# The last 96 rows of w2 in 24 small transfers on partitions 0 to 31

## The chip, the cores and the metric

The kernel runs on one core of a Trainium2 chip. The metric is the device time of one execution in microseconds (us). Times of single executions, the profiled one among them, are compared with the median of several.

## What is computed

One decode step for two sequences: attention of 32 heads over a cache of 4096 positions, a two-layer network with relu beside it, and a gate that mixes the two.

```python
x = A_x                                             # [2, 1, 512]
g = sigmoid((x * gate_w).sum(-1, keepdims=True))
q = (x @ wq), 32 heads of 128
p = softmax(q @ k_cache.T / sqrt(128))              # k_cache, v_cache [2, 32, 4096, 128]
a = (p @ v_cache), heads joined, @ wo               # wo [4096, 512]
b = relu(x @ w1) @ w2                               # w1 [512, 1376], w2 [1376, 512]
out = g * a + (1 - g) * b
```

All inputs are bfloat16. The two caches are 64 MB each; w2 is 1.4 MB.

## The kernel before

**Streaming.** The caches are read in eight units of 8 MB each (64 KB on each of 128 partitions). Unit 0 and unit 7 of K come as halves, unit 7 of V too. Nearly all loads are issued by SP, in one queue, in the order of the code: w1, wq, ten transfers of K (L272), nine of V (L282), wo in two parts (L283, L284), then w2. Two one-off loads (x, two rows, and gate_w, one row) are issued by ACT (L265, L266). A K or V transfer waits until the buffer that it fills is read out. Every load increments a semaphore by 16 when it has landed.

**Stages.** `gate` makes the gate's values g and 1 - g (`gm`). `q_proj` makes q. `ffn_h` makes the hidden layer h on PE in eleven groups of four matmuls, each 128 hidden units by 2 sequences, from w1 in `kt`; DVE then applies relu and the factor 1 - g and writes `hT` (128 partitions x 11 groups x 2). Then 64 pieces of K are transposed by DVE (`k_turn`, L383) and multiplied by PE (`k_scores`, L404 and its helper L197). `softmax` follows; E and ET lie in `kt`. `spread(j)` writes the weights of job j into `ptm`, in four parts, on POOL, DVE and ACT; `v_unit(j)` multiplies them with V on PE; `v_extract(j)` brings the sum out on DVE into `X2[:, j]`. `o_gather` collects the heads, `project` multiplies with wo, and `wo_sum` adds its four parts to the result's PSUM tile `fin`.

**w2.** The 1376 hidden units are put on partitions as follows: units 0 to 1279 as ten groups (partition p has units 10p to 10p + 9), and an eleventh group from the last 128 units, 1248 to 1375. Its first 32 are there twice, so POOL sets `hT[0:32, 10, :]` to zero (L376). w2 comes in six transfers, all with 128 partitions: `w2a` (L285) is the eleventh group, 1 KB on each partition. It waits for the four parts of the last `spread`, `pt_8_0` to `pt_8_3`, for then `kt` is no longer read. `w2b` to `w2f` (L290) are the ten groups in five parts: 6144, 2560, 512, 512 and 512 bytes on each partition, with no wait of their own.

**The end.** After `project`, PE runs `ffn_f(10)` (the eleventh group, waits for `w2a`), `wo_sum`, `ffn_f(0)` to `ffn_f(7)` (waits for `w2b` at 0 and `w2c` at 6), half of group 8, and `ffn_last`, which waits for `w2d`, `w2e` and `w2f` in turn. Four copies by DVE and ACT (L576, L578) bring the result to `out_sb`, and SP writes it out (L292). SP's queue holds nothing else.

The engines run in the order in which the code adds to them; a wait holds up all that follows on its engine.

## Time and profile before

| | us |
|---|---|
| median of 3 runs (lowest, highest) | 344.14 (343.99, 344.16) |
| profiled execution, its own time | 344.06 |
| its span, first to last instruction | 342.8 |
| PE busy | 197.6 (58%) |
| DVE busy | 178.6 (52%) |
| ACT, POOL busy | 23.1, 19.9 |
| w2a, from issue to last landing | 30.4 |
| w2b to w2f, the same | 31.5 to 32.3 |

The span is the time between the first and the last instruction in the trace; the rest of the execution's time, 1.3 us, lies around it. A slice is a fortieth of the span, 8.6 us. A transfer is issued by an instruction on SP or ACT and then moved by sixteen DMA engines, each of which takes its share of the rows; the time from issue to landing holds the wait behind transfers that were issued earlier. The trace has a record for every packet (queue, start, duration, bytes, but not which of the sixteen engines) and for every increment of a semaphore, so the sixteen landings of a transfer can be seen one by one.

### The profile page before, as it was taken

The page shows a single profiled execution, that of the slowest core. Times are in us where ns is not written, and L with a number is a line of the kernel's source. Part 1 is how long each engine was busy: PE and PEld are TensorE (multiplying, and loading weights), DVE is VectorE, ACT ScalarE, POOL GpSimd, SP SyncE. Part 2 cuts the span into 40 slices and gives each one's busy share as a digit, 9 for nine tenths or more (in the row PEclk, how much of TensorE's full clock was granted, in tenths as well). Part 3 has the DMA queues.
Part 4 walks back from the last instruction along what each step waited for, and adds up shares of the span by engine and source line. Part 5 has one row for each costly group of instructions (what it writes and reads, how often), then busy time and mean ns, then how long its engine had stood idle before and what let it go on. Part 6 is the DMA issues. An engine that isn't in the chain of part 4 may idle for free.

```text
span 342.8 us, 2538 instructions
## 1 busy us (share of the span) xinstructions
PE 197.6 (58%) x1228; PEld 54.5 (16%) x972; DVE 178.6 (52%) x127; ACT 23.1 (7%) x71; POOL 19.9 (6%) x36
## 2 busy tenths in 40 slices
PE   0177329799969799699799337220706043150656
PEld 0141001111111111111111013100303011020231
DVE  2239059899799899698999562220100103020121
ACT  1040000000000000000000250000000000000000
POOL 8000000000000000000000040110100101000000
PEclk9999959989999999989999858755656758565787
DMA  8998989899998999998999999999999999999996
GB/s 348 428 489 369 482 375 482 382 474 451 400 489 375 422 444 467 392 459 386 471 436 428 461 398 417 449 459 413 444 413 446 421 436 451 405 468 390 425 404 243
DMA packets 4196, 145.61 MB, mean 425 GB/s; under 512 B 469, under 2 KB 986, under 8 KB 1242
## 3 DMA queue, kind: packets, MB, share of 16 engines
q1 hardware_dynamic: 4180, 145.46, 98.6%
q8 instruction: 8, 0.13, 0.2%
q14 instruction: 2, 0.02, 0.0%
q10 hardware_dynamic: 6, 0.00, 0.0%
HBM read 145.46 MB, written 0.00 MB: 424 GB/s over the span
## 4 chain that ended last, share of the span: by engine, by line
DMA 68%; DVE 15%; PE 13%; ACT 1%; issue 1%; POOL 0%; SPq 0%; DVEq 0%
DMA kv<-in_A_k_cache_dram 31%; DMA kv<-in_A_v_cache_dram 23%; DVE kt L383 13%; DMA kt<-in_B_w_dram 9%; PE PS L458 6%; DMA kv<-in_A_wq_dram 4%; PE PS L404 3%; PE PS L197 3%; ACT kt L425 1%; PE PS L330 1%; DVE mpad L410 1%; DVE kt L468 1%; POOL ptm L441 0%; DVE qbuf L464 0%; DVE kt L429 0%
## 5 line engine op out<-in xcount | busy, mean ns | idle before, releaser
L383 DVE STREAM_TRANSPOSE kt<-kv 128x2048 f32<-128x2048 f32 x64 | 141.2, 2274 | 22.4 <-DMA kv<-in_A_k_cache_dram 22.3
L404 PE MATMUL PS<-kt,qbuf 128*128 128x512 bf16 x256 | 105.7, 413 | 31.8 <-DVE kt L383 26.3
L197 PE MATMUL PS<-kt,qbuf 128*128 128x512 bf16 x256 | 105.1, 411 | 0.0
L458 PE MATMUL PS<-kv,ptm 128*32 128x512 bf16 x512 | 46.4, 539 | 79.2 <-DMA kv<-in_A_v_cache_dram 76.2
L464 DVE TENSOR_TENSOR qbuf<-PS,maskc 128x512 f32<-128x512 f32 x9 | 6.2, 692 | 109.0 <-PE PS L458 109.0
L404 PEld LDWEIGHTS PS<-kt,qbuf 128*128 128x128 bf16 x256 | 25.5, 100 | 139.9 <-DVE kt L383 72.8
L458 PEld LDWEIGHTS PS<-kv,ptm 128*32 128x32 bf16 x512 | 19.0, 129 | 105.1 <-issue 98.2
L441 POOL COPY ptm<-kt 32x512 bf16<-32x512 bf16 (+1 forms) x18 | 11.5, 638 | 268.5 <-DVE rsum L472 175.6
L357 ACT ACTIVATE qbuf<-PS 32x8 bf16<-32x8 bf16 x40 | 7.9, 196 | 134.0 <-PE PS L197 132.6
L445 ACT ACTIVATE ptm<-kt 32x512 bf16<-32x512 bf16 (+1 forms) x9 | 5.3, 604 | 99.9 <-PE PS L458 98.6
L468 DVE TENSOR_REDUCE kt<-qbuf 128x128 f32<-128x512 f32 x9 | 9.2, 1026 | 0.3
L425 ACT ACTIVATE kt<-PS,negm 128x512 bf16<-128x512 f32 x8 | 5.4, 700 | 30.5 <-DVE negm L421 30.5
L330 PE MATMUL PS<-kv,xTw 128*32 128x512 bf16 x32 | 3.6, 631 | 5.8 <-DMA kv<-in_A_wq_dram 5.8
L475 PE MATMUL PS<-rsum,sell 128*32 128x1 f32 x4 | 0.4, 197 | 10.1 <-DVE rsum L472 10.1
L429 DVE STREAM_TRANSPOSE kt<-kt 128x1024 bf16<-128x1024 bf16 x4 | 5.0, 1245 | 1.7 <-ACT kt L425 1.4
L345 DVE CAST qrow<-PS 128x256 bf16<-128x256 f32 x2 | 2.4, 1400 | 6.4 <-PE PS L330 6.4
L505 PE MATMUL PS<-kv,oW 128*2 128x512 bf16 x32 | 3.5, 603 | 1.3 <-DMA kv<-in_A_wo_dram 1.3
L297 PE MATMUL PS<-ident,x_sb 3*128 3x3 bf16 x4 | 0.3, 165 | 6.0 <-POOL s L227 6.0
L483 PE MATMUL PS<-kt,selx 128*32 128x128 f32 x18 | 3.3, 325 | 0.4 <-DVE kt L468 0.4
L230 POOL MEMSET ptm<- 128x4096 bf16 x1 | 3.5, 3501 | 0.0
L300 DVE COPY xT<-PS 128x12 bf16<-128x12 bf16 x1 | 0.2, 171 | 6.3 <-PE PS L297 6.3
L410 DVE TENSOR_REDUCE mpad<-PS 128x1 f32<-128x2048 f32 x1 | 2.3, 2293 | 2.2 <-PE PS L197 2.2
(64 smaller groups left out, 44.5 us busy)
## 6 DMA issues: line engine op xcount, KB each, us to landing
kv<-in_A_k_cache_dram SPq DMA_DIRECT2D x4, 4096.0 KB, 31.6
kv<-in_A_v_cache_dram SPq DMA_DIRECT2D x2, 4096.0 KB, 27.0
kv<-in_A_wq_dram SPq DMA_DIRECT2D x1, 4096.0 KB, 14.9
kv<-in_A_wo_dram SPq DMA_DIRECT2D x1, 3072.0 KB, 29.3
kt<-in_B_w_dram SPq DMA_DIRECT2D x1, 1376.0 KB, 5.7
kv<-in_A_wo_dram SPq DMA_DIRECT2D x1, 1024.0 KB, 31.4
kt<-in_B_w_dram SPq DMA_DIRECT2D x1, 768.0 KB, 31.9
kt<-in_B_w_dram SPq DMA_DIRECT2D x1, 320.0 KB, 32.3
```

What stands on the lines that cost most here:

```text
L197: return e.add_instruction(mybir.InstMatmult(start_tensor_calc=start, stop_tensor_calc=stop, tile_size=(128, 128), tile_position=(0, 0), l ...
L330: pe(lambda e, n=n, t=t: e.matmul(psf(32 * (n % 4), 32 * (n % 4) + 32, (QR_B + n // 4) * BANK, 512), lhsT=xTw[:, t, :], rhs=wq_sb[:, t, n ...
L357: act(lambda a, hq=hq: a.activation(out=qbuf[32 * hq:32 * hq + 32, g % 2, :, :, 32 + 32 * hq], in_=cols[32 * hq:32 * hq + 32, u4 // 2, 2 * ...
L383: dve(lambda v: v.transpose(out=dst, in_=pairs[:, h, 64 * rr:64 * rr + 64]), waits=([f"pe_sc_{i - NKT}"] if i >= NKT else ["pe_h"] if i == ...
L404: return e.matmul(args[0], lhsT=args[1], rhs=args[2], start=first, stop=last)
L410: dve(lambda v: v.tensor_reduce(out=mpad[:, 0:1], in_=psf(0, 128, 0, 2048), axis=AX.X, op=ALU.max), waits=["pe_sc_63", "c_mpad"], signal=" ...
L425: act(lambda a, bk=bk, e2=e2: a.activation(out=blocks[:, bk, :, 16 * e2:16 * e2 + 16], in_=psf(0, 128, bk * BANK, 512).rearrange("p (r n) ...
L441: pool(lambda e, args=args: e.tensor_copy(**args), waits=waits, signal=f"pt_{j}_{hq}")
L445: act(lambda e, args=args: e.activation(func=ACT.Copy, **args), waits=waits, signal=f"pt_{j}_{hq}")
L458: pe(lambda e, m=m, t=t: e.matmul(psf(32 * t, 32 * t + 32, V_B[j % 2] * BANK, 512), lhsT=ptm[:, j % 2, 4 * m:4 * m + 4, :, :], rhs=rows[:, ...
L464: dve(lambda e: e.tensor_tensor(out=Y.rearrange("p (c d) -> p c d", c=4), in0=psf(0, 128, V_B[u % 2] * BANK, 512).rearrange("p (c d) -> p ...
L468: dve(lambda e: e.tensor_reduce(out=X2[:, u, :], in_=Y.rearrange("p (c d) -> p d c", c=4), axis=AX.X, op=ALU.add), waits=[f"dve_y{u}"], si ...
```

## The change

The eleventh group is replaced by the last 96 units alone, 1280 to 1375, in four groups on fewer partitions: 32 units (1280 to 1311), twice 24 (the even and the odd ones of 1312 to 1359), and 16 (1360 to 1375). `hT` grows to 14 groups. Their w2 rows come in 24 transfers in place of `w2a`: eight with 4 partitions of 1 KB (partitions o, o + 8, o + 16, o + 24), eight with 3 partitions of 2 KB, and eight with 2 partitions of 1 KB. All increment `w2a`'s semaphore, and PE waits for 24 times 16. The first waits as `w2a` did. In bytes they are 96 KB in place of 128 KB. `w2b` to `w2f` are as they were, and stand behind them in SP's queue.

With this, `ffn_h` has 56 matmuls for 44 and four DVE instructions for two; POOL's memset is gone; `ffn_f` runs for groups 10 to 13 ahead of `wo_sum`, with 32, 24, 24 and 16 partitions. As w2's place in `kt` grows, five of the nine parts of `X2` move to a buffer of their own, and the result's staging tile takes the place of x.

```diff
+H_TAIL = ((32, 1280, 1), (24, 1312, 2), (24, 1313, 2), (16, 1360, 1))
...
-    hT = sb("hT", [128, 11, 2], dt.bfloat16)
-    out_sb = sb("out_sb", [2, 512], dt.bfloat16)
+    hT = sb("hT", [128, 14, 2], dt.bfloat16)
+    X2a = sb("X2a", [128, 5, 128], dt.float32)
+    out_sb = x_sb[0:2, :]
...
-    w2f = flat[:, 0:2816].bitcast(dt.bfloat16)
+    w2f = flat[:, 0:3584].bitcast(dt.bfloat16)
...
-    X2 = flat[:, 2944:4096].rearrange("p (u d) -> p u d", d=128)
+    X2b = flat[:, 3584:4096].rearrange("p (u d) -> p u d", d=128)
...
-    sp(lambda e: e.dma_start(w2[:, 10, :], B_w2[1248:1376, :]).then_inc(sem["w2a"], 16),
-       waits=[f"pt_8_{hq}" for hq in range(4)])
-
+    ready = [f"pt_8_{hq}" for hq in range(4)]
+    few = []
+    for r, n, row in ((10, 32, 1280), (11, 24, 1312), (13, 16, 1360)):
+        w = 2 if r == 11 else 1
+        src = B_w2[row:row + n * w, :].rearrange("(p w) n -> p (w n)", w=w)
+        few += [(w2f[o:n:8, 512 * r:512 * (r + w)], src[o:n:8, :]) for o in range(8)]
+    for i, (dst, src) in enumerate(few):
+        sp(lambda e, dst=dst, src=src: e.dma_start(dst, src).then_inc(sem["w2a"], 16), waits=ready if i == 0 else [])
...
+    def h_rows(r):
+        return 128 if r < 10 else H_TAIL[r - 10][0]
+
     def ffn_h():
-        for ft in range(11):
+        for ft in range(14):
             for t in range(4):
                 def fn(e, ft=ft, t=t):
                     o = t * DFF
-                    cols = w1[:, o + ft:o + 1280:10] if ft < 10 else w1[:, o + 1248:o + 1376]
-                    return e.matmul(psf(0, 128, H_C0 + 2 * ft, 2), lhsT=cols, rhs=xT3[:, t, 0:2], start=(t == 0), stop=(t == 3))
+                    n, c0, step = (128, ft, 10) if ft < 10 else H_TAIL[ft - 10]
+                    return e.matmul(psf(0, n, H_C0 + 2 * ft, 2), lhsT=w1[:, o + c0:o + c0 + (n - 1) * step + 1:step], rhs=xT3[:, t, 0:2],
+                                    start=(t == 0), stop=(t == 3))
...
-        pool(lambda g: g.memset(hT[0:32, 10, :], 0.0), waits=["dve_h0", "dve_h1"], signal="c_h10")
+        for i, (r0, r1) in enumerate(((0, 10), (10, 11), (11, 13), (13, 14))):
+            n = h_rows(r0)
+            dve(lambda v, r0=r0, r1=r1, n=n: v.scalar_tensor_tensor(
+                out=hT[0:n, r0:r1, :], in0=psf(0, n, H_C0 + 2 * r0, 2 * (r1 - r0)).rearrange("p (r b) -> p r b", b=2), scalar=0.0,
+                in1=gm[0:n, :].unsqueeze(1).to_broadcast([n, r1 - r0, 2]), op0=ALU.max, op1=ALU.mult),
+                waits=["pe_h", "dve_gm"], signal=f"dve_h{i}")
...
     def ffn_f(r, first=False, groups=4):
-        dw = {10: [(sem["w2a"], 16)], 0: [(sem["w2b"], 16)], 6: [(sem["w2c"], 16)]}.get(r, [])
+        dw = {10: [(sem["w2a"], 384)], 0: [(sem["w2b"], 16)], 6: [(sem["w2c"], 16)]}.get(r, [])
+        n = h_rows(r)
...
     ffn_f(10, first=True)
+    for r in (11, 12, 13):
+        ffn_f(r)
     wo_sum()
```

## The prediction

> **What bounds the kernel now.** I read the page's 40 slices first, then the DMA issues, then SP's own queue, then the end of the chain of waits.

> ```profile
> DMA  8998989899998999998999999999999999999996
> q1 hardware_dynamic: 4180, 145.46, 98.6%
> q10 hardware_dynamic: 6, 0.00, 0.0%
> HBM read 145.46 MB, written 0.00 MB: 424 GB/s over the span
> ```

> The sixteen DMA engines are busy from the first slice to the last but one: 145 MB at 424 GB/s is the whole span. No compute engine matters unless it makes a transfer start late or lengthens what follows the last landing.

> ```profile
> 300.00:337.00 37.00, 17.60 (x186) 7.79 (x178) 6.01 (x9) 0.43 (x1) 0.81 (x2) 0.68 0.98 420
> 337.00:338.90 1.90, 1.40 (x18) 0.23 (x12) 0.55 (x1) 0.00 (x0) 0.00 (x0) 0.62 0.94 361
> 338.90:341.00 2.10, 1.60 (x48) 0.70 (x48) 0.34 (x2) 0.20 (x1) 0.00 (x0) 1.00 0.35 119
> ```

> The last two figures of a window are DMA share and GB/s. From 338.9 the share is 0.35: the engines do not stop together. The semaphore records of the last transfer (sem_w2f) say the same: of its sixteen landings, one for each engine, seven lie from 338.9 to 339.6 and nine from 340.2 to 340.9. The last one counts; the early engines have up to 2.0 us to spare.

> ```profile
> 308.00 32.27 DMA kt<-in_B_w_dram
> 340.26 0.04 issue
> 340.31 0.33 PE PS L513 x10
> 340.64 0.55 PE PS L208 x6
> 341.19 0.02 issue
> 341.21 0.28 DVE out_sb L576
> ```

> The chain ends in a w2 transfer, then a tail of matmuls, copies and the output transfer: 1.9 us from the last landing (340.9) to the end of the span (342.8). The change does not touch that tail.

> ```profile
> 305.86 0.43 SPq L284 DMA_DIRECT2D kv<-in_A_wo_dram  x1
> 307.15 0.33 SPq L285 DMA_DIRECT2D kt<-in_B_w_dram  x1
> 307.52 1.86 SPq L290 DMA_DIRECT2D kt<-in_B_w_dram  x4
> L290 SPq DMA_DIRECT2D kt<-in_B_w_dram x5: 432/432/8858, 307.5 to 309.4; - x5
> ```

> This is the view that decides. SP issues w2 early, 30 us ahead of its data, one transfer every 0.475 us. But the fifth L290 issue, begun at 309.42, takes 8.858 us instead of 0.432: it ends at 318.28. It has no wait of its own, so SP's queue was full. Nine transfers were then outstanding: V unit 6, the half unit of job 8, wo0, wo1, w2a, w2b, w2c, w2d, w2e. Unit 6's last landing is at 317.7, the next one's at 327.4. So the tenth went when the ninth before it had gone. Before, this costs nothing: 318.28 is still 20 us ahead of the data.

> **The change, part by part.**

> *Fewer bytes.* The old w2a, 8 packets of 1 KB on each engine, goes. wo1 and w2a land 0.3 to 0.4 us apart on an engine (first landings 335.3 and 335.6, last 337.2 and 337.6), so an engine that gets none of the new rows gains 0.35 us. The 96 rows come on few engines: the two rows of x and the one of gate_w made six packets on q10, a data and a semaphore packet for each row, so a transfer of 4, 3 or 2 rows runs on 4, 3 or 2 engines. If these are always the same, one engine takes at most 8 x 1 + 8 x 2 + 8 x 1 = 32 KB: 16 packets of 0.046 us, 8 of about 0.083 (between 0.046 for 1 KB and 0.24 for 6 KB) and 24 semaphore packets of 0.015, 1.75 us, net +1.4. Following the packets end to end (each starts within 12 ns of the end of the one before), the engine that carried the gate row ends 2.0 us before the last one; 1.4 fits. [...]

> *Twenty-three more issues on SP, ahead of w2b to w2f.* Without a limit they cost 23 x 0.475 = 10.9 us of SP, and w2b would be issued at 318.5, still 19 us early: nothing. With the limit as a count of transfers, they do cost. The first five small ones go by 309.4. The sixth waits for unit 6 (317.7), the seventh for the half unit (327.4), the eighth for wo0 (334.7). wo1 is all that is left then, and lands from 335.3 on. From 334.8 the other seventeen follow at SP's pace. For one of them I take 0.37 us, from the issue of the output transfer, also of two rows (0.323, and 0.045 between issues): 17 x 0.37 = 6.3, to 341.1. w2b's issue ends at 341.6; from SP's first issue (w1, ended 1.13) to its first packet (1.75) it is 0.6, so w2b's data begin at 342.2. w2b to w2f take 3.3 us of engine time (last landings: w2a 337.6, w2f 340.9), hence 345.5, and 0.5 from an engine's last packet to its landing: 346.0 against 340.9, **+5.1 us**. The engines stand idle meanwhile, which no other work can fill, as nothing else is queued. Bounds: an issue costs between 0.275 (gate_w's on ACT, 0.229 and 0.045) and 0.475, -1.6 to +1.8; the eighth may go when wo0 leaves the early engines (332.8), -2.0, and the ninth may have to wait for wo1's last landing (337.2), +2.1. Together +1.5 to +9.0; I keep +2.5 to +7, as the ends need two of these at once.

> *PE and DVE early.* ffn_h has 56 matmuls for 44: 44 took 2.60 us, so +0.71. Four DVE instructions for two of 0.23, and no POOL memset (0.09, nobody waits for it): some +0.3. On DVE the first transpose (25.84) is queued behind them: 1.0 late at most, and with it the next K issue (34.76). Hidden: two K units are queued then, to 65.8, and the transposes wait 22.3 us for K in all. Uncovered it would be +1.0.

> *PE late.* ffn_f(10) to (13) are 16 matmuls for 4, between 338.08 and the wait for YW that ends at 339.09. A group of 24 took 0.51, so +0.25; at most 12 x 0.08 = 1.0 (four alone took 0.32). Either is over by the landing of w2b (339.5): nothing. The moves of X2, hT and out_sb change no duration.

> **Sum.** The profiled execution took 344.06 (span 342.8; the median of the runs is 344.14): 344.06 + 5.1 = **349.2 us**.

> **Rivals.**

> 1. *Not slower: the queue's limit is one of descriptors.* A 128-row transfer is nine packets on an engine (eight rows and a semaphore), a small one two. At the block an engine held some 77, and 72 when it opened, so 81 would be the limit; 24 small ones are 48, and with the 27 of three large transfers 75. All would go by about 319, w2b to w2f well before 336, and the late engines save w2a: 344.06 - 0.35 = 343.7. For it: nothing in the trace separates count from descriptors. Against: eight waiting and one running is the simpler reading, and 81 happens to be nine nines. It is also the case in which the change does what it says.

> 2. *The new rows fall on a late engine.* Nine of sixteen landings are late, and I could place one engine only. With 1.4 on a late one: 340.9 + 1.4, 345.5 us.

> 3. *Each small transfer costs its engines a fixed time.* w2d, w2e and w2f, 64 KB each, land 0.2 us apart, which bounds it above for packets already small (512 B): 24 x 0.2 = 4.8, less 0.35 and the 2.0 of slack, +2.4: 346.5 us. Against: the semaphore packets show 9 ns. [...]

> **How the numbers follow.** The count of nine: 0.54. Rival 1: 0.28, rivals 2 and 3: 0.08 each, something else 0.02. The measurement can tell about 0.2%, 0.7 us, from no change; rival 1 gains less, and reaches 0.7 only if w2a cost twice its 0.35, so I put 0.24 of it on no difference and 0.04 on faster; with half of the rest, faster 0.05, same 0.25, slower 0.70. The likeliest case alone spans 346.5 to 351. The range takes in rival 1 below, 343.6, and ends at 350.8.

> **What would show it.** Right: SP's issues of the small rows stall at the sixth, seventh and eighth, L290's come after 340, and the slices show the DMA share falling before the last 5 us. Rival 1: all issues over by about 336 and the last landings near 340.5. Rival 2: issues in time, but a few landings of w2f after 341.5. Rival 3: issues in time, and the small rows' last landing seconds the w2f delay, 2 us or more after wo1's. The early part is wrong if the first K issues shift the landing of V units.

## The result and the profile after

| | before | after |
|---|---|---|
| median, us | 344.12 (343.99 to 344.18, 6 runs) | 346.34 (346.10 to 346.48, 6 runs) |
| ratio | | 1.0064, 95% interval 1.0051 to 1.0077 |
| span of the profiled execution, us | 342.8 | 345.0 |

The change makes the kernel 2.2 us slower, 0.64%. The forecast was slower by 5.1.

The head of the page after, its 40 slices of DMA, the main queue and what was read:

```profile
span 345.0 us, 2610 instructions
...
DMA  8998999999898999999999998999999999999994
...
q1 hardware_dynamic: 4180, 145.43, 98.1%
...
HBM read 145.43 MB, written 0.00 MB: 422 GB/s over the span
```

The 0.03 MB are saved, and the span is 2.2 us longer. The last slice but one is still full; the last falls from 6 to 4.

The windows of the changed kernel at its end (the last two columns are DMA share and GB/s):

```profile
300.00:337.00 37.00, 17.33 (x185) 7.53 (x178) 6.00 (x9) 0.43 (x1) 0.81 (x2) 0.68 0.99 417
337.00:338.90 1.90, 1.48 (x16) 0.10 (x8) 0.28 (x1) 0.00 (x0) 0.00 (x0) 0.67 0.97 325
338.90:341.00 2.10, 0.34 (x19) 0.22 (x21) 0.41 (x1) 0.00 (x0) 0.00 (x0) 1.00 0.54 182
341.00:343.10 2.10, 1.74 (x50) 0.99 (x48) 0.00 (x0) 0.00 (x0) 0.00 (x0) 0.66 0.13 41
343.10:345.00 1.90, 0.28 (x6) 0.00 (x0) 0.56 (x2) 0.54 (x2) 0.00 (x0) 0.50 0.00 1
```

Until 337 nearly all is as before (417 GB/s for 420). From 337.0 to 338.9 the share is 0.97, but the engines move 325 GB/s in place of 361; from 338.9 to 341.0 the share is 0.54 for 0.35. The last issue of w2 ends at 334.0, so the engines are not waiting for transfers to be issued: they are busy longer. From the last landing (343.1) to the end it is 1.9 us, as before.

The sixteen landings of four transfers, from the semaphore records (w2a has 72 landings now: 24, 24, 16 and 8 on four engines, if the rows of every transfer fall on the same ones in turn):

```
before  wo1   335.3 335.4 335.4 335.6 335.6 335.8 335.9 336.6 336.9 336.9 337.0 337.0 337.1 337.1 337.2 337.2
        w2f   338.9 339.1 339.1 339.3 339.3 339.6 339.6 340.2 340.5 340.5 340.6 340.6 340.7 340.7 340.8 340.9
after   wo1   335.4 335.5 335.6 335.6 335.6 335.9 336.4 336.5 337.2 337.3 337.3 337.3 337.3 337.4 337.6 337.7
        w2a   335.8 336.0 336.1 ... 340.3 340.3 340.4 340.6
        w2b   337.5 337.8 337.8 337.9 339.1 339.2 339.2 339.2 339.2 339.3 339.5 339.5 339.5 339.6 341.3 341.7
        w2f   339.0 339.2 339.3 339.3 340.5 340.6 340.6 340.6 340.7 340.7 340.8 340.9 340.9 341.0 342.7 343.1
```

Two engines are behind all others, with w2b at 341.3 and 341.7 and w2f at 342.7 and 343.1. By that count they are the two that took 24 of the small transfers each: from 338.6 on w2a's landings come in two rows, 0.16 to 0.19 us apart in each, as of two engines. The last of them is at 340.6, some 5 us after wo1 on an early engine. The other late engines end at 341.0 as before: they did not keep what w2a had cost them.

SP's issues of the small transfers and of w2b to w2f, in the changed kernel (durations in ns: least, median, most):

```profile
L294 SPq DMA_DIRECT2D kt<-in_B_w_dram x24: 567/579/730, 307.1 to 322.1; - x24
its engine sat idle before it (us, times) until:
who waited for it (us, times):
  PEld PS L528: 2.8, 1
  PE PS L528: 2.1, 1
```

```profile
L297 SPq DMA_DIRECT2D kt<-in_B_w_dram x5: 432/568/8772, 322.7 to 333.6; - x5
```

All 24 went without a stall, from 307.1 to 322.7, though the half V unit and wo were outstanding with them. One of the five L297 issues took 8.772 us: w2d, from 324.28 to 333.05. That is still some 5 us ahead of its first packet (337.9). The PE lines show a wait of 2.1 us for the small rows, which delays nothing, as w2b lands a microsecond later still.

The end of the chain of waits, changed kernel:

```profile
322.12 0.57 SPq L294
...
322.73 18.95 DMA kt<-in_B_w_dram
...
341.72 0.81 PE PS L528 x24
342.56 0.48 PE PS L528 x8
...
343.50 0.29 DVE x_sb L593
```

The chain runs through SP's issues back to 307, but these are ahead of the data: the step that holds the time is the transfer that starts at 322.73 and lands 18.95 us later.

### The profile page after: what moved, and what is told of

It is laid out like the page before. It is cut to its first block, busy times and chain, and to the rows that moved or that the text cites. A ratio compares the mean times of both kernels' runs of the same rounds, so it can differ in the third digit from the quotient of the medians.

```text
span 345.0 us, 2610 instructions
## 1 busy us (share of the span) xinstructions
PE 199.4 (58%) x1252; PEld 54.7 (16%) x996; DVE 178.1 (52%) x129; ACT 23.1 (7%) x71; POOL 19.9 (6%) x35
## 3 DMA queue, kind: packets, MB, share of 16 engines
q1 hardware_dynamic: 4180, 145.43, 98.1%
## 4 chain that ended last, share of the span: by engine, by line
DMA 72%; DVE 14%; PE 8%; SPq 4%; issue 1%; DVEq 0%
DMA kv<-in_A_v_cache_dram 31%; DMA kv<-in_A_k_cache_dram 31%; DVE kt L394 14%; DMA kt<-in_B_w_dram 5%; PE PS L469 4%; DMA kv<-in_A_wq_dram 4%; SPq L294 4%; PE PS L337 1%; PE PS L415 1%; PE PS L199 1%; PE PS L528 0%; DVE kt L482 0%; DVE qbuf L478 0%; DVE x_sb L593 0%; SPq L269 0%
## 5 line engine op out<-in xcount | busy, mean ns | idle before, releaser
L456 ACT ACTIVATE ptm<-kt 32x512 bf16<-32x512 bf16 (+1 forms) x9 | 5.3, 603 | 100.0 <-PE PS L469 98.6
L489 PE MATMUL PS<-rsum,sell 128*32 128x1 f32 x4 | 0.4, 197 | 10.1 <-DVE rsum L486 10.1
L482 DVE TENSOR_REDUCE X2a<-qbuf 128x128 f32<-128x512 f32 x5 | 5.2, 1031 | 0.2
L482 DVE TENSOR_REDUCE kt<-qbuf 128x128 f32<-128x512 f32 x4 | 4.1, 1022 | 0.1
```

The lines of the kernel that those rows point to most:

```text
L456: act(lambda e, args=args: e.activation(func=ACT.Copy, **args), waits=waits, signal=f"pt_{j}_{hq}")
L482: dve(lambda e: e.tensor_reduce(out=x2(u), in_=Y.rearrange("p (c d) -> p d c", c=4), axis=AX.X, op=ALU.add), waits=[f"dve_y{u}"], signal=f ...
```

## The experiments

Two theories stood after the result. **A**: each transfer costs each engine that it uses a fixed time, about 0.2 us, whatever it carries. **B**: the bytes, 32 KB on two engines and a few partitions, are the cost. Durations of single packets are from the trace's packet records; "slow" is a packet of w2b (6 KB, of which each run has 128) that takes over 0.26 us, where 0.24 is normal. Where many small transfers stand ahead of w2b, its packets also wait behind these on their own engine (they take up to 0.92 us in the changed kernel, and 1.9 to 2.5 in e1), so the last column tells of something else only from e2 down.

| run | what | us | ratio (95%) | slow w2b packets |
|---|---|---|---|---|
| before | | 344.12 | | 1 |
| after | 24 small transfers | 346.34 | 1.0064 (1.0051, 1.0077) | 45 |
| e1 | w2a in 24 on all engines | 347.91 | 1.0107 (1.0092, 1.0123) | 35 |
| e8 | w2a in 12 on all engines | 345.90 | 1.0050 (1.0037, 1.0064) | 54 |
| e3 | 24, half the bytes | 346.03 | 1.0053 (1.0039, 1.0066) | 13 |
| e4 | 12 ahead of wo1, 12 behind | 346.35 | 1.0063 (1.0049, 1.0076) | 36 |
| e2 | 8 on 3 engines | 344.67 | 1.0014 (1.0006, 1.0023) | 49 |
| e5 | the same, other partitions | 344.15 | 0.9999 (0.9990, 1.0008) | 3 |
| e6 | one of 96 rows | 344.52 | 1.0010 (1.0001, 1.0019) | 60 |
| e11 | w2a in two halves | 344.70 | 1.0014 (1.0005, 1.0023) | 71 |
| e7 | before without w2a | 343.84 | 0.9990 (0.9981, 0.9998) | 0 |
| e10 | after without its 24 | 343.82 | 0.9989 (0.9980, 0.9998) | 0 |
| e12 | 4 on 3 engines | 344.06 | 0.9995 (0.9986, 1.0004) | 0 |

The kernel before, run beside e1 to e4 on the same chip, had 344.21, beside e5 to e8 344.17, beside e10 to e12 344.23.

**e1: as many transfers, no pile.** On the kernel before:

```diff
-    sp(lambda e: e.dma_start(w2[:, 10, :], B_w2[1248:1376, :]).then_inc(sem["w2a"], 16), ...)
+    few = [(w2[16 * o:16 * o + 16, 10, c0:c1], B_w2[1248 + 16 * o:1264 + 16 * o, c0:c1])
+           for o in range(8) for c0, c1 in ((0, 128), (128, 256), (256, 512))]
```

> The kernel before with the old w2a's 128 rows in 24 transfers of 16 partitions and a part of the row each (256, 256 and 512 B): the same bytes on each of the sixteen engines as before, nothing piled up, only the number of transfers as in the changed kernel. Theory A (each transfer costs each engine that it uses about 0.2 us, whatever its bytes, once some twelve are queued): 24 x 0.2 = 4.8 less the 0.35 that w2a took, on all engines, late ones too: about 348.5 us. Theory B (the cost is the 32 KB and their rows piled on two engines and 32 partitions): within 0.4 of before, 344.5 at most.

347.91 us: A. The windows of this run:

```profile
300.00:337.00 37.00, 16.23 (x190) 7.25 (x182) 6.00 (x9) 0.43 (x1) 0.81 (x2) 0.73 1.00 410
337.00:339.00 2.00, 1.27 (x12) 0.10 (x8) 0.21 (x1) 0.00 (x0) 0.00 (x0) 0.50 1.08 98
339.00:341.00 2.00, 0.00 (x0) 0.00 (x0) 0.48 (x1) 0.00 (x0) 0.00 (x0) 0.50 0.79 243
```

From 337 to 339 the engines are fully busy and move 98 GB/s. What is counted as busy is not bytes: sixteen packets of w2b, as many as there are engines, take 1.9 to 2.5 us each, for 0.24. PE has nothing to do from 339 to 341.

**e8: half as many.** The same with 32 partitions to a transfer, 12 in all:

```diff
-           for o in range(8) ...   w2[16 * o:16 * o + 16, ...]
+           for o in range(4) ...   w2[32 * o:32 * o + 32, ...]
```

> The run of w2a in 24 transfers on all engines (347.91 us) with 12: 32 partitions and a part of the row each, same bytes. Theory A, each transfer 0.2 us, none absorbed: 12 x 0.2 - 0.35 = +2.05, 346.2 us. If some twelve are absorbed in a queue: 344.5 us or less.

345.90 us. By the medians the twelve that are left out are worth 2.01 us, 0.168 each, and the first twelve, against the kernel without w2a (e7, 343.84), 2.06, or 0.17 each. The semaphore records give the price directly: the landings of successive small transfers on one engine come 0.18 us apart in both runs, as a mean over the engines.

That the two steps are equal does not show that nothing is absorbed. The profiled execution of e8 is already 0.7 us late when the half V unit has landed (328.1, for 327.4 in the kernel before), ahead of all these transfers. From the last landing of wo0 to the last of w2f it is 5.8 us in e7, 7.4 in e8 and 10.1 in e1: 1.6 for the first twelve and 2.7 for the second. And w2b lands 1.1 us behind the last small transfer in both runs, for 1.9 behind w2a before, so some 0.7 us of the pile is hidden, once.

**e3: half of the bytes**, each small transfer cut to 512 bytes on a partition:

```diff
-        sp(lambda e, dst=dst, src=src: e.dma_start(dst, src)...
+        sp(lambda e, dst=dst, src=src: e.dma_start(dst[:, 0:256], src[:, 0:256])...
```

> The changed kernel with each of the 24 transfers cut to 512 bytes on a partition; the other bytes of these rows are left out, 48 KB in place of 96 KB. Theory A: same number of transfers, same time as the changed kernel, 346.3 us. Theory B: half of the pile or less, 345.2 us or less.

346.03 us. A's number was 346.3, B's at most 345.2. What half of the bytes are worth, 0.3 us, is within the two intervals.

**e4: twelve ahead of wo1.**

```diff
     for i, (dst, src) in enumerate(few):
+        if i == 12:
+            sp(... wo1 ...)
```

> The changed kernel with twelve of the 24 transfers issued ahead of wo1 and twelve behind it; same transfers, same bytes. Theory A, if a burst of some twelve is absorbed and worked off under wo1's 8 KB packets: half of the cost goes, 344 to 345.2 us. If every transfer holds its engine for 0.2 us wherever it stands, or by theory B: 346.3 us.

346.35 us: the same as in one row. Putting half of the transfers ahead of wo1 gains nothing; their cost is not worked off beside wo1's packets.

**e2: eight transfers, the same pile.** H_TAIL becomes four groups of 24 units; partition p of group r has unit 1280 + 24r + p. The 96 rows come in 8 transfers of 3 partitions, with 4 rows of 1 KB on each: if the same three engines take them all, as e12's landings show it for its four transfers (they come in three rows), 32 packets of 1 KB or 32 KB to an engine.

```diff
+    rows4 = B_w2[1280:1376, :].rearrange("(r p) n -> p r n", r=4)
+    few = [(w2[o:24:8, 10:14, :], rows4[o:24:8, :, :]) for o in range(8)]
```

> [...] Theory A: 8 transfers are absorbed (8 x 0.2 = 1.6 hides under 32 x 0.046 = 1.5); the pile then ends inside the early engines' 2.0 us and the late engines keep the 0.35 saved: 343.8 us. Theory B: as many bytes on two engines as in the changed kernel and more on the third: 346.3 us.

344.67 us: some 1.7 of the 2.2 are gone, with 32 KB on each of three engines by that count. A is right and B is not, but 343.8 was not reached. The trace shows why not in w2b's packets: 49 of 128 are slow, up to 0.51 us. Three loaded engines have 24 of the 128, eight each, so at least 25 slow packets are on engines that carry none of the new rows. A third thing is at work, and it asks for a theory **C**: the small rows land on partitions that other engines write at the same time. Its rival **D** is that few engines with many small packets slow the rest wherever these land.

**e5: other partitions, nothing else.** The eight transfers of e2 go to partitions o, o + 4, o + 8 for o = 0 to 3 and 32 to 35, in place of o, o + 8, o + 16. The author took these for partitions that the loaded engines themselves write in the large transfers ("own" in the expectation of e12); the trace names neither an engine nor its partitions, so this is not shown.

```diff
-    few = [(w2[o:24:8, 10:14, :], rows4[o:24:8, :, :]) for o in range(8)]
+    few = [(w2[o:o + 9:4, 10:14, :], rows4[i:24:8, :, :]) for i, o in enumerate((0, 1, 2, 3, 32, 33, 34, 35))]
```

> [...] The matmuls still read partitions 0 to 23, so the product of the last 96 units is not computed from its rows. Theory C (what is left of the delay is a collision of writes with other engines' partitions): back to 343.8 us. Theory D (it is the rows themselves, small packets from few engines, wherever they land): 344.6 us as before the edit.

344.15 us, and 3 slow packets for 49, with the same transfers and the same bytes. D is out: where the rows land counts. C fits, but that it is the writes of other engines that collide with them is not shown. The windows of e2 and of e5 (first two lines e2's):

```profile
337.00:339.00 2.00, 0.92 (x24) 0.31 (x24) 0.46 (x1) 0.00 (x0) 0.00 (x0) 1.00 0.95 314
339.00:341.00 2.00, 1.59 (x44) 0.92 (x46) 0.23 (x1) 0.00 (x0) 0.00 (x0) 0.61 0.57 195
```

```profile
337.00:339.00 2.00, 1.12 (x32) 0.41 (x32) 0.69 (x1) 0.00 (x0) 0.00 (x0) 1.00 0.92 361
339.00:341.00 2.00, 1.34 (x48) 0.70 (x40) 0.00 (x1) 0.00 (x1) 0.00 (x0) 0.80 0.42 133
```

From 337 to 339 e5 moves 361 GB/s (the kernel before 355 in the same window) and e2 314; from 339 to 341 e2 has the rest still to do, a share of 0.57 for 0.42. The bytes are the same in both. The intervals of the two times just overlap; the packets, 49 slow ones against 3, leave no doubt that the partitions matter.

The 343.8 of theory C was not reached either. The last two landings of w2f, 340.76 and 340.90, stand behind the others (to 340.57). They are probably loaded engines that had too little to spare; the records do not name them.

**e6 and e11: slow packets without any pile.** e6 has one transfer of 96 rows, six to an engine if sixteen share them evenly, with the rest of the change; e11 is the kernel before with w2a in two halves of 64 partitions: the same bytes, one transfer more.

```diff
+    few = [(w2[0:96, 10, :], B_w2[1280:1376, :])]                       # e6, H_TAIL = ((96, 1280, 1),)
```

```diff
+    for i in range(2):                                                  # e11
+        sp(lambda e, i=i: e.dma_start(w2[64 * i:64 * i + 64, 10, :], B_w2[1248 + 64 * i:1312 + 64 * i, :])...
```

> The changed kernel with its 96 rows as one group on 96 partitions in one transfer, 6 rows on each of the sixteen engines: 24 transfers undone, the rest of the change (the compute, the moves of X2, hT and out_sb, 32 KB less) kept. If all of the time is in the transfers: 344.1 us (2 rows of 0.046 less on each engine, -0.09). If the rest of the change costs: above 344.4.

> [...] By the cost of a transfer alone (0.17): 344.3 us, with w2b's packets at 0.24 us as before. If writes to other engines' partitions also collide (theory C): some 40 or more of w2b's 128 packets over 0.26 us, and 344.5 us.

344.52 and 344.70 us, with 60 and 71 slow packets. e6 alone looked as if the rest of the change cost something; e10 says that it does not. e11 has one transfer more than the kernel before, 0.17 by e8, and lost 0.5. That theory C reaches these two runs was the author's assumption: which engine writes which of their rows is not shown. e11 even writes the partitions and bytes of the kernel before, with 71 slow packets for 1. What is measured is that one transfer of 96 rows, or two of 64, is enough to slow the large packets that follow.

**e7 and e10: what there was to save, and what the rest costs.** e7 is the kernel before with the load of w2a left out, e10 the changed kernel without its 24 transfers.

```diff
-    sp(lambda e: e.dma_start(w2[:, 10, :], ...).then_inc(sem["w2a"], 16), ...)                    # e7
-    for i, (dst, src) in enumerate(few): ...                                                     # e10
```

> The kernel before with the load of w2a left out; the product of the eleventh group is taken from what the buffer held. It measures the term of the sum for the late engines, -0.35: 343.85 us if the landings follow the bytes. If it is nearer 344.2, there was nothing to save.

> The changed kernel with its 24 transfers left out and all else kept (the moves, the 56 matmuls, the order at the end); the last 96 units are multiplied with what the buffer held. If all of the time is in the transfers: as the kernel before without w2a, 343.84 us. If the 344.52 of the single 96-row transfer came from the rest of the change: 344.2 us or more.

343.84 and 343.82 us. 0.33 to 0.41 us is all that the last rows of w2 cost in the kernel before, so no placing of them can gain more. The rest of the change, more matmuls and other buffers, costs nothing.

**e12: a version without either cost.** On the kernel before:

```diff
+    tail = B_w2[1280:1376, :].rearrange("(p r) n -> p (r n)", r=8)
+    for o in range(4):
+        sp(lambda e, o=o: e.dma_start(ET[o:o + 9:4, :], tail[o:12:4, :]).then_inc(sem["w2a"], 16), ...)
```

The last 96 units make eight groups of 12; `ffn_h`, `hT` and `ffn_f` follow.

> A version that should keep what the change was after: the kernel before with the last 96 rows in 4 transfers of 3 partitions (o, o + 4, o + 8), 8 rows of 1 KB next to each other on each, in ET's place, which is free by then. On each of three early engines 4 packets of 8 KB (0.31 us each) and 4 transfers: 1.3 us in place of 0.35. If transfers cost 0.17 and own partitions don't collide: the late engines decide, 343.85 us. If the three engines are not early enough, or collisions remain: 344.2 us or more.

344.06 us beside 344.23, ratio 0.9995 with an interval that holds 1: no difference that can be told. Two windows of its end:

```profile
337.00:338.90 1.90, 1.15 (x40) 0.53 (x40) 0.69 (x1) 0.00 (x0) 0.00 (x0) 1.00 0.94 365
338.90:341.00 2.10, 1.66 (x48) 0.81 (x48) 0.12 (x1) 0.13 (x1) 0.00 (x0) 0.79 0.40 129
```

They move 365 and 129 GB/s, as the kernel before does (361 and 119), and no packet is slow. Its w2f lands to 340.9, for 340.8 in e7 and 340.9 in the kernel before, while wo0, ahead of all of this, lands to 335.0 in this profile and to 334.7 in that of before. From wo0's last landing to w2f's it is 5.9 us, for 5.8 in e7 and 6.2 in the kernel before. That would be nearly all there was to gain, but one profile cannot place a difference of this size; the 0.3 that there is to gain is about what the runs of one kernel differ by.

The landings of this run also say what kind of cost the 0.17 is. The twelve come in three rows, 0.31 us apart in each, and one packet of 8 KB takes 0.31: here a transfer costs its data and no more. In e5, with four packets of 0.046 us to a transfer, they come 0.20 apart. So 0.17 to 0.18 is the least distance between two landings on one engine, not something added to every transfer.

## Why the prediction was wrong

**The sign was right by luck: the mechanism that was put first was not at work.** The step that failed is the one that was said to decide: that SP's queue holds nine transfers, so that the sixth small one waits and the rest follow too late. 24 small ones went one after the other while three large ones were outstanding, and then w2b and w2c. The nine was read from one stall, and the same stall fits a limit in packets, which is what rival 1 said. e1 supports it, with two packets of each small transfer on every engine:

```profile
L289 SPq DMA_DIRECT2D kt<-in_B_w_dram x24: 341/420/2886, 306.0 to 319.8; - x24
L293 SPq DMA_DIRECT2D kt<-in_B_w_dram x5: 432/879/8772, 322.2 to 334.9; - x5
```

The 22nd to 24th small transfer and w2b behind them stall there, for 2.89, 1.17, 2.39 and 2.39 us. With the 0.04 to the next issue, 2.39 is twice one packet of the half V unit (1.213). The number at which the limit lies was not measured. Rival 1 was right on SP, and wrong that nothing else would cost.

**The price of a small transfer on its engine was mis-sized.** The sum had 1.75 us for 24 of them, by the recorded packets (0.046, 0.083 and 0.015). The packet records do not show the landings: the first eight packets follow each other by 0.048, while the landings on a loaded engine come 0.17 to 0.18 us apart, up to the last (340.27, 340.44, 340.62). For 24 that is 4.1 to 4.3. This is rival 3, with its price from the distance of w2d, w2e and w2f in the trace before. Its mechanism holds for transfers as small as these. Its time, 346.5 for 346.34 measured, is closer than its terms: the 0.2 was a bound from 64 KB transfers, and the 2.0 to spare is that of the earliest engine alone. It had 0.08 because the semaphore packets show 9 ns, which turned out to say nothing of the landing.

**What held.** The bound and the tail: 1.9 us from the last landing to the end in both kernels. The saving of 0.35 on an engine that loses w2a: 0.33 in e7. That the small rows fall on early engines, by the count of landings: of the seven engines that ended early, four still do, two are the loaded ones and one has joined the late group; the late ones end where they did. Rival 2 is out. That ffn_h's twelve further matmuls are hidden: the fourth K issue comes at 35.03 for 34.76, the half V unit lands at 327.5 for 327.4, and e10 is as fast as e7.

**What no step had.** The late engines gained nothing, as large packets beside the small rows were slowed: 25 of wo1's 128 packets take over 0.33 us, up to 0.425, for at most 0.321 before. The last landings of wo0 and wo1 lie 2.90 us apart for 2.52, and that uses up what w2a had cost. e2 against e5 (49 slow packets of w2b for 3) shows that such packets depend on the partitions that are written; for the changed kernel itself it is argued. It does not set its time: these engines end at 341.0, 2 us ahead of the two loaded ones.

The parts add up roughly: 24 x 0.17 = 4.1, less w2a's 0.35 and the 2.0 us that the earliest engine had to spare, is 1.7, and 2.0 with 0.18. What is missing to 2.2 stays open. The engine that ends last may have had less to spare: the seven early landings of w2f before lie from 338.9 to 339.6, 2.0 to 1.3 ahead of the last.

## What to carry to other kernels

When the DMA engines are the bound, count the transfers that each engine takes, not only its bytes: here small ones landed 0.17 to 0.18 us apart on an engine, down to parts of 256 bytes on a partition (e1), so pieces that took an engine less than that were paid for as if they did. Before moving work to engines that are early, measure what there is to gain by leaving the work out (here 0.33 to 0.41 us), and try the same rows on other partitions: here the same eight transfers slowed 49 large packets of 128 on one set of partitions and 3 on another, and only a run told which. A single stall of a queue says that there is a limit, not in what it is counted.
